# When tables are loaded and placed at the start of a fused Fourier mixer and feed-forward kernel

## The chip, the cores and the metric

The kernel runs on one core of a Trainium2 chip. The metric is the device time of one execution in microseconds. Before the change it is 861.91 us (median of three runs, 861.05 to 862.39). The core has five instruction streams that run side by side and wait for each other by semaphores: TensorE (matmul, "PE" in the profile), VectorE ("DVE"), ScalarE ("ACT"), GpSimd ("POOL") and SyncE ("SP"), which only issues transfers. GpSimd issues transfers too, among them those that convert 32-bit floats to 16-bit ones on the way. Sixteen DMA engines carry them all.

## What is computed

Two layers: a mixer that works in the frequency domain along the sequence, and a feed-forward network on its output.

```python
# x: (8, 3008, 256); w_r, w_i: (256, 256); b_r, b_i: (256,)
X = np.fft.rfft(x, axis=1)
Yr = Xr @ w_r - Xi @ w_i + b_r
Yi = Xr @ w_i + Xi @ w_r + b_i
Yr = sign(Yr) * maximum(abs(Yr) - 0.01, 0)     # the same for Yi
y = np.fft.irfft(Yr + 1j * Yi, n=3008, axis=1)
# then, on all 24064 rows; w_in: (256, 2048), w_out: (2048, 256); s, b: one number each
r = maximum(y @ w_in, 0)
out = (s * (r * r) + b) @ w_out
```

The kernel makes the Fourier transform of length 3008 = 94 x 32 out of matmuls with constant tables: a transform of length 94 (table A), one of length 32 with twiddle factors (table F, one 128 x 128 block for each of 24 pairs of frequencies), and, for the way back, one of length 32 (table T, 24 blocks too) and one of length 94 (table C).

## The kernel before

Image 0 is treated by a routine of its own, `first_batch`, which keeps all in on-chip memory. The later images go through units of work that are spread between the matmuls of the feed-forward network. A helper, `evac`, copies a PSUM tile to on-chip memory by ScalarE or VectorE, whichever has less to do by a running count. What comes first in the text comes first in each engine's stream, except where the scheduler of the language moves it.

The loads are issued in this order. `F_c` and `T_c` are the tables F and T as they lie in memory, 384 KB each; `F_t`, `F_2` and `T_t` are what the matmuls read, with zeros between the blocks.

```python
A_t = cpool.tile([P, 96], F16, name="A_t")
nc.sync.dma_start(out=A_t[0:N1, :], in_=A_d)
emit_load_x(0)                       # four chunks of image 0, issued by GpSimd, f32 -> f16
...                                  # w_st: w_r and w_i, 256 KB each, SyncE; b_g: four rows of 1 KB
F_c = uspool.tile([P, NPAIR, 2, N2], F16, name="F_c", tag="us")
nc.sync.dma_start(out=F_c.rearrange("p q r k -> p q (r k)"), in_=F_d)
...                                  # b_h: two rows, GpSimd
T_c = uspool.tile([P, NPAIR, 64], F16, name="T_c", tag="us")
nc.sync.dma_start(out=T_c, in_=T_d)
nc.sync.dma_start(out=sel_t, in_=S_d)
nc.sync.dma_start(out=eye_t, in_=E_d)
nc.sync.dma_start(out=C_t, in_=C_d)
b_st = rpool.tile([P, 2, D], F32, name="b_st", tag="rt")
for i, bv in enumerate((b_r, b_i)):
    nc.sync.dma_start(out=b_st[:, i], in_=bv.unsqueeze(0).to_broadcast([P, D]))
...                                  # s_bc, bb_bc
```

The pool of `b_st` and the two `w_st` has three buffers, which the feed-forward network's `rt` tiles use later. The small work and the placing of tables:

```python
def make_bounds():                   # GpSimd: low, high <- b_st
    for t, c in ((low, -LAM), (high, LAM)):
        nc.gpsimd.tensor_scalar(out=t, in0=b_st, scalar1=-1.0, scalar2=c, op0=ALU.mult, op1=ALU.add)

def make_w_g():                      # GpSimd: W_g <- w_st, used by images 1 to 7
    nc.gpsimd.tensor_tensor(out=W_g[:, :, 1], in0=w_st[1], in1=w_st[0], op=ALU.subtract)
    nc.gpsimd.tensor_tensor(out=W_g[:, :, 0], in0=w_st[1], in1=w_st[0], op=ALU.add)
    nc.gpsimd.tensor_scalar_mul(out=W_g[:, :, 0], in0=W_g[:, :, 0], scalar1=-1.0)

def place_f():
    for a in range(2):
        r = slice(64 * a, 64 * a + 64)
        nc.scalar.copy(out=blocks(F_t)[r, :, :, a], in_=F_c[r])
        for h, f in enumerate(F_2):
            q = slice(h * H, h * H + H)
            nc.vector.tensor_scalar_mul(out=blocks(f)[r, :, 0, a], in0=F_c[r, q, 1], scalar1=-1.0)
            nc.vector.tensor_copy(out=blocks(f)[r, :, 1, a], in_=F_c[r, q, 0])

def place_t():
    for i in range(4):
        r = slice(32 * i, 32 * i + 32)
        c = 64 * (i % 2)
        nc.vector.tensor_copy(out=T_t[r, :, c : c + 64], in_=T_c[r])
```

`first_batch` reads the chunks as they come, then runs twelve steps, (ec, u) with ec the half of the features and u = 0..5 (written (ec, u) = 0..11 in a row here):

```python
for c in range(N2 // XCH):           # 4 chunks
    for dc in range(DC):
        ...                          # 8 matmuls x16 x A_t -> psh   (L328)
        ...                          # two evac: one on ScalarE, one on VectorE -> ut
    keep_awake(18 if c < 3 else 12)  # matmuls on ones, to keep TensorE busy
    if c == 2:
        place_w()                    # ScalarE: W_t <- w_st
with tc.issue_after(last_dve.ins), tc.issue_after(last_act.ins):
    place_f()
    place_t()
gate = nc.gpsimd.tensor_copy(out=w_in_t[0][0:1, 0:1], in_=T_c[0:1, 0, 0:1])
with tc.issue_after(gate.ins):
    emit_load_x(1)
    emit_load_weights()              # w_in, w_out
...
def mix(ec, u):       # 8 matmuls ut x W_t -> psh (L367); then
    ...               # u % 3 == 1: g = copy on ScalarE (bias comes later, by a matmul with sel_t and b_h)
    ...               # else: g = psh + b_g on VectorE, the "bias add" (L377)
def fwd_dft(ec, u):   # 8 matmuls F_t, F_2 x g -> psf (L398); m on ScalarE (L403), z on VectorE (L405)
def inv_dft(ec, u):   # 4 matmuls z x T_t -> psa (L416); evac -> vt
...
for i in range(2 * U + 2):           # U = 6
    ...                              # mix(step i), fwd_dft(step i-1), inv_dft(step i-2)
    ...                              # from i = 8 on: turn, last_dft -> yt, and image 1's first stage
    if i == 6:
        make_w_g()
        make_bounds()
```

After that, the main loop runs the feed-forward network of all images (first matmul L702, relu L709 -> `rt`, square L713 or L716 -> `gt`, second matmul L771, last scaling L781), with the mixer's units of images 1 to 7 between.

Of the kernel before, what the change touches and what calls it, by code (L numbers as in the profile page):

```python
# [14 lines left out]
P = 128  # L15
# [79 lines left out]
def kernel(  # L95
# [13 lines left out]
    nc = tc.nc  # L109
    B, S, D = x.shape  # L110
# [5 lines left out]
    H = NPAIR // 2  # L116
# [5 lines left out]
    F_d = nc.inline_tensor(fwd.astype(np.float16), name="dft_fwd").ap()  # L122
    T_d = nc.inline_tensor(inv.astype(np.float16), name="dft_inv").ap()
    C_d = nc.inline_tensor(last.astype(np.float16), name="dft_last").ap()
# [3 lines left out]
    E_d = nc.inline_tensor(np.eye(P).astype(np.float16), name="identity").ap()  # L128
    S_d = nc.inline_tensor(sel.astype(np.float16), name="bias_sel").ap()
# [23 lines left out]
    def evac(dst, src, cols, scale=None):  # L153
        ta, td = 0.17 + cols / 1200.0, 0.15 + cols / 960.0
        if load["act"] + ta <= load["dve"] + td:
            load["act"] += ta
            if scale is None:
                return None, nc.scalar.copy(out=dst, in_=src)  # L158
            return None, nc.scalar.mul(out=dst, in_=src, mul=scale)
        load["dve"] += td  # L160
        if scale is None:
            return nc.vector.tensor_copy(out=dst, in_=src), None
        return nc.vector.tensor_scalar_mul(out=dst, in0=src, scalar1=scale), None

    def two_banks():
        return hpool.tile([P, 2, 512], F32, name="psh", tag="psh")
# [4 lines left out]
    def other_bank():  # L171
        return apool.tile([P, 512], F32, name="psa", tag="psa")
# [17 lines left out]
    def keep_awake(n):  # L190

        ps = other_bank()
        for _ in range(n):
            nc.tensor.matmul(ps[:, 0:P], ones, ones, start=True, stop=True)
# [15 lines left out]
        for i, bv in enumerate((b_r, b_i)):  # L210
            nc.sync.dma_start(out=b_g[r : r + 1, i], in_=bv.unsqueeze(0))
    F_c = uspool.tile([P, NPAIR, 2, N2], F16, name="F_c", tag="us")
    nc.sync.dma_start(out=F_c.rearrange("p q r k -> p q (r k)"), in_=F_d)
    b_h = cpool.tile([P, D], F16, name="b_h")
    nc.vector.memset(b_h, 0.0)

# [1 line left out]
        nc.gpsimd.dma_start(out=b_h[64 * i : 64 * i + 1], in_=bv.unsqueeze(0))  # L218
    sel_t = cpool.tile([P, P], F16, name="sel_t")
    T_c = uspool.tile([P, NPAIR, 64], F16, name="T_c", tag="us")  # L220
    nc.sync.dma_start(out=T_c, in_=T_d)

    nc.sync.dma_start(out=sel_t, in_=S_d)
    eye_t = cpool.tile([P, P], F16, name="eye_t")
    nc.sync.dma_start(out=eye_t, in_=E_d)
    C_t = cpool.tile([96, 96], F16, name="C_t")
    nc.sync.dma_start(out=C_t, in_=C_d)

    b_st = rpool.tile([P, 2, D], F32, name="b_st", tag="rt")
    for i, bv in enumerate((b_r, b_i)):  # L230
        nc.sync.dma_start(out=b_st[:, i], in_=bv.unsqueeze(0).to_broadcast([P, D]))
    low = cpool.tile([P, 2, D], F16, name="low")
    high = cpool.tile([P, 2, D], F16, name="high")
    W_g = cpool.tile([P, DC, 2, D], F16, name="W_g")
    s_bc = cpool.tile([P, 1], F32, name="s_bc")
    bb_bc = cpool.tile([P, 1], F32, name="bb_bc")
    nc.sync.dma_start(out=s_bc, in_=moe_s.unsqueeze(0).to_broadcast([P, 1]))
    nc.sync.dma_start(out=bb_bc, in_=moe_b.unsqueeze(0).to_broadcast([P, 1]))

    w_in_t = [cpool.tile([P, DFF], F16, name=f"w_in_{dc}") for dc in range(DC)]  # L240
    w_out_t = cpool.tile([P, MC, D], F16, name="w_out_t")
# [14 lines left out]
    T_t = cpool.tile([P, NPAIR, P], F16, name="T_t")  # L256
    nc.vector.memset(T_t, 0.0)
    F_2 = [uspool.tile([P, H, P], F16, name="F_2", tag="us") for _ in range(2)]
# [3 lines left out]
    def make_bounds():  # L262
        for t, c in ((low, -LAM), (high, LAM)):
            nc.gpsimd.tensor_scalar(
                out=t, in0=b_st, scalar1=-1.0, scalar2=c, op0=ALU.mult, op1=ALU.add
            )

    def make_w_g():
# [6 lines that stand above are left out]
    def blocks(t):  # L275
        return t.rearrange("p q (r a k) -> p q r a k", r=2, a=2)

    def place_w():
        for i in range(2):
            nc.scalar.copy(out=W_t[:, :, i], in_=w_st[i])  # L280

    def place_f():
        for a in range(2):
            r = slice(64 * a, 64 * a + 64)
            nc.scalar.copy(out=blocks(F_t)[r, :, :, a], in_=F_c[r])

            for h, f in enumerate(F_2):
                q = slice(h * H, h * H + H)
                nc.vector.tensor_scalar_mul(
                    out=blocks(f)[r, :, 0, a], in0=F_c[r, q, 1], scalar1=-1.0  # L290
                )
                nc.vector.tensor_copy(out=blocks(f)[r, :, 1, a], in_=F_c[r, q, 0])

    def place_t():
        for i in range(4):
            r = slice(32 * i, 32 * i + 32)
            c = 64 * (i % 2)
            nc.vector.tensor_copy(out=T_t[r, :, c : c + 64], in_=T_c[r])  # L298

    def make_bias():  # L300
        ps = other_bank()
# [17 lines left out]
    def first_batch():  # L319
        ut = ypool.tile([P, DC, 96, N2], F16, name="ut", tag="yt")  # L320
        last_dve = last_act = None
        keep_awake(44)
        for c in range(N2 // XCH):
            for dc in range(DC):
                ps = two_banks()
                for j in range(XCH):
                    lo = j * D + dc * P
                    last_pe = nc.tensor.matmul(  # L328
                        ps[:, j // 4, (j % 4) * 96 : (j % 4) * 96 + 96],
                        x16[(0, c)][0:N1, lo : lo + P], A_t[0:N1, :],  # L330
                        start=True, stop=True,
                    )
                for h in range(2):
                    n2 = c * XCH + 4 * h
                    on_dve, on_act = evac(
                        ut[:, dc, :, n2 : n2 + 4],
                        ps[:, h, 0:384].rearrange("p (n k) -> p k n", k=96), 384,
                    )
                    last_dve = on_dve or last_dve
                    last_act = on_act or last_act  # L340
            with tc.issue_after(last_pe.ins):
                keep_awake(18 if c < 3 else 12)
            if c == 2:
                with tc.issue_after(last_act.ins):
                    place_w()
        with tc.issue_after(last_dve.ins), tc.issue_after(last_act.ins):
            place_f()
            place_t()

        gate = nc.gpsimd.tensor_copy(out=w_in_t[0][0:1, 0:1], in_=T_c[0:1, 0, 0:1])  # L350
        with tc.issue_after(gate.ins):
# [5 lines left out]
        vt = bigpool.tile([P, DC, N2, 96], F16, name="vt", tag="corr")  # L357
        gs = {}
        zt = {}
        g_last = [None]  # L360

        def mix(ec, u):
            ps = two_banks().rearrange("p h (j r e) -> p (h j) r e", j=2, r=2)
            for j in range(4):
                q = 4 * u + j
                for dc in range(DC):
                    nc.tensor.matmul(  # L367
                        ps[:, j], ut[:, dc, 4 * q : 4 * q + 4, :],
                        W_t[:, dc, :, ec * P : (ec + 1) * P],
                        start=(dc == 0), stop=(dc == DC - 1),  # L370
                    )
            g = vpool.tile([P, 4, 2, P], F16, name="g0", tag="v")
            if u % 3 == 1:
                nc.scalar.copy(out=g, in_=ps)
                load["act"] += 1.02
            else:
                g_last[0] = nc.vector.tensor_tensor(  # L377
                    out=g, in0=ps,
                    in1=b_g[:, :, ec * P : (ec + 1) * P].unsqueeze(1).to_broadcast([P, 4, 2, P]),
                    op=ALU.add,  # L380
                )
                load["dve"] += 1.2
            gs[(ec, u)] = g
# [77 lines left out]
        def some(n):  # L461
            for _ in range(n):
                if more:
                    more.pop(0)()

        steps = [(ec, u) for ec in range(DC) for u in range(U)]
        for i in range(2 * U + 2):
            if i < 2 * U:
                mix(*steps[i])
            if 0 <= i - 1 < 2 * U:  # L470
                fwd_dft(*steps[i - 1])
            if 0 <= i - 2 < 2 * U:
                inv_dft(*steps[i - 2])
            k = i - U - 2
            if 0 <= k < 4:
                turn(0, k)
            if 0 <= k - 1 < 4:
                last_dft(0, 8 * (k - 1))
            if i >= 2 * U:
                some(3)  # L480
            if i == 6:
                make_w_g()
                make_bounds()
        for k in range(4):
            turn(1, k)
            some(1)
# [307 lines left out]
    def schedule(start, span, units):  # L794
        for i, u in enumerate(units):
            plan.setdefault(start + (i * span) // len(units), []).append(u)

    more = first_batch()
    load.update(act=0.0, dve=0.0)
    mark = {}  # L800
# [8 lines left out]
    for b in range(2, B):  # L809
        s0, s1, s2 = mark[b - 2], mark[b - 1], mark[b]  # L810
        p = s1 - s0
        schedule(s0 + 40, p - 48, s1_units(b))
        p = s2 - s1
# [47 lines left out]
```

## Time and profile before

| What | Value |
|---|---|
| Time, median of three | 861.91 us |
| Span in the profile | 860.5 us |
| PE busy | 839.1 us, 98% |
| PE weight loads busy | 604.3 us, 70% |
| DVE busy | 699.4 us, 81% |
| ACT busy | 642.8 us, 75% |
| POOL busy | 33.2 us, 4% |
| DMA moved | 95.07 MB, mean 110 GB/s |

The busy table is a sum over the whole span. The page's second part cuts the span in 40 slices of 21.5 us and gives each engine's busy share in tenths, TensorE's granted clock and the load of the DMA engines. The chain is followed back from the last instruction, at each step to what released it. A timeline row reads: start in us, length in us, engine, line of the program, operation, output<-inputs, count, and in brackets the idle time before with what ended it.

### The profile page before, as it was taken

How to read it: one execution, taken by the hardware profiler on the slowest of the kernel's cores; microseconds unless marked ns; L12 is line 12 of the kernel's file. 1: busy time of each engine (PE TensorE's matmuls, PEld its weight loads, DVE VectorE, ACT ScalarE, POOL GpSimd, SP SyncE). 2: the span in 40 equal slices, each digit the busy share in tenths (PEclk: the TensorE clock that was granted, in tenths of full speed). 3: DMA queues.
4: the chain of work that ended last, by engine and by line, in shares of the span. 5: the costliest groups of instructions: out<-in, count | busy, mean ns of one | idle time of the engine just before them, and what ended most of it. 6: DMA issues, size and time to landing. Idle time of an engine off the chain costs nothing.

```text
span 860.5 us, 17125 instructions
## 1 busy us (share of the span) xinstructions
PE 839.1 (98%) x6690; PEld 604.3 (70%) x6690; DVE 699.4 (81%) x1019; ACT 642.8 (75%) x856; POOL 33.2 (4%) x53
## 2 busy tenths in 40 slices
PE   6889999999999999999999999999999999999996
PEld 6666776777777766777667776777767777766665
DVE  6688997888878887888878888888977888776664
ACT  4587887777877887778777877788877787766662
POOL 4110000000000000000000000000000000000000
PEclk9899999999999999999999999999999999999999
DMA  8845266423673357423664246713354223411111
GB/s 183 138 93 144 77 150 179 141 69 70 157 179 110 84 136 179 141 73 75 169 157 115 76 108 166 193 42 94 102 154 117 63 77 96 111 32 38 37 40 53
DMA packets 104866, 95.07 MB, mean 110 GB/s; under 512 B 9422, under 2 KB 97234, under 8 KB 103442
## 3 DMA queue, kind: packets, MB, share of 16 engines
q1 hardware_dynamic: 98786, 79.57, 31.9%
q0 software_dynamic: 6000, 14.42, 10.4%
q8 instruction: 52, 0.85, 0.4%
q14 instruction: 28, 0.23, 0.1%
HBM read 52.54 MB, written 46.66 MB: 115 GB/s over the span
## 4 chain that ended last, share of the span: by engine, by line
PE 89%; DVE 4%; ACT 3%; DMA 2%; issue 1%; SPq 0%; POOL 0%; DVEq 0%; POOLq 0%
PE psh L702 36%; PE psa L771 36%; PE psf L568 4%; PE psf L503 3%; PE psf L539 2%; PE psf L554 2%; PE psf L598 2%; PE psf L651 2%; DMA x<-in_x_dram 1%; DVE gt L716 1%; ACT rt L709 1%; PE psh L367 1%; DVE T_t L298 1%; ACT yt L158 1%; ACT m L403 0%
## 5 line engine op out<-in xcount | busy, mean ns | idle before, releaser
L709 ACT ACTIVATE rt<-psh 128x1024 f32<-128x1024 f32 (+2 forms) x384 | 387.1, 1009 | 117.0 <-PE psh L702 115.8
L716 DVE TENSOR_TENSOR gt<-rt 128x1024 f16<-128x1024 f32 (+2 forms) x323 | 386.2, 1198 | 101.0 <-ACT rt L709 100.4
L771 PE MATMUL psa<-w_out_t,gt 128*128 128x256 f16 (+1 forms) x3024 | 453.9, 272 | 0.1
L771 PEld LDWEIGHTS <-gt 128*128 128x128 f16 (+1 forms) x3024 | 301.1, 101 | 186.9 <-issue 1.7
L702 PE MATMUL psh<-yt,w_in 128*128 128x512 f16 (+1 forms) x1344 | 396.9, 378 | 0.0
L702 PEld LDWEIGHTS <-w_in 128*128 128x128 f16 x1536 | 142.8, 98 | 26.6 <-issue 1.7
L781 DVE SCALAR_TENSOR_TENSOR ost<-psa,s_bc,bias_bc 128x512 f32<-128x512 f32 (+1 forms) x96 | 70.8, 737 | 8.1 <-PE psa L771 5.7
L713 ACT ACTIVATE gt<-rt 128x1024 f16<-128x1024 f32 (+2 forms) x61 | 64.3, 1054 | 1.0
L573 DVE TENSOR_TENSOR ring<-psf,s 128x512 f16<-128x512 f32 x84 | 57.4, 683 | 3.5 <-PE psf L568 3.3
L158 ACT CAST v<-psf 128x512 f16<-128x512 f32 x80 | 46.5, 582 | 18.1 <-PE psf L598 18.1
L158 ACT CAST xf<-psf 128x512 f16<-128x512 f32 x82 | 48.0, 585 | 11.1 <-PE psf L539 11.1
L158 ACT CAST u<-psf 96x512 f16<-96x512 f32 x78 | 45.1, 580 | 12.3 <-PE psf L503 12.1
L702 PE MATMUL psh<-tail,w_in 128*128 128x512 f16 (+1 forms) x192 | 52.1, 353 | 0.0
L568 PE MATMUL psf<-W_g,xf 128*128 128x256 f16 x336 | 50.4, 273 | 0.0
L158 ACT CAST yt<-psf 128x480 f16<-128x480 f32 (+2 forms) x76 | 38.5, 518 | 14.4 <-PE psf L651 14.4
L503 PE MATMUL psf<-x,A_t 94*96 94x512 f16 x104 | 39.6, 381 | 1.7 <-ACT yt L158 0.5
L579 DVE TENSOR_TENSOR ring<-ring,high 128x512 f16<-128x512 f16 x84 | 35.5, 422 | 2.2
L580 DVE TENSOR_TENSOR ring<-ring 128x512 f16<-128x512 f16 x84 | 35.4, 421 | 1.9
L578 DVE TENSOR_TENSOR ring<-ring,low 128x512 f16<-128x512 f16 x84 | 35.3, 421 | 1.5
L568 PEld LDWEIGHTS <-xf 128*128 128x128 f16 x336 | 32.9, 98 | 3.7
L182 POOL DMA_DIRECT2D x<-in_x_dram x32 | 16.7, 524 | 482.3 <-PE psf L503 445.1
L651 PE MATMUL psf<-C_t,vs 96*128 96x96 f16 x448 | 32.9, 205 | 0.0
(80 smaller groups left out, 496.9 us busy)
## 6 DMA issues: line engine op xcount, KB each, us to landing
out_dram<-ost SPq DMA_DIRECT2D x152, 128.0 KB
x<-in_x_dram POOLq DMA_DIRECT2D x32, 376.0 KB, 6.0
ud<-u SPq DMA_DIRECT2D x28, 384.0 KB
us<-ud SPq DMA_DIRECT2D x28, 384.0 KB
vd<-v SPq DMA_DIRECT2D x42, 256.0 KB
vs<-vd SPq DMA_DIRECT2D x14, 768.0 KB
ring<-ring SPq DMA_DIRECT2D x280, 32.0 KB
out_dram<-ost SPq DMA_DIRECT2D x16, 120.0 KB
```

The costliest lines, as they stand in the source:

```text
L158: return None, nc.scalar.copy(out=dst, in_=src)
L503: nc.tensor.matmul(ps[0:96, :], A_t[0:N1, :], x16[(b, c)][0:N1, j * D : (j + 2) * D], start=True, stop=True,)
L568: nc.tensor.matmul(ps[:, r, :], xt[:, 2 - r, dc], W_g[:, dc, r], start=(dc == 0), stop=(dc == DC - 1),)
L573: nc.vector.tensor_tensor(out=t, in0=ps, in1=hold[i // 2][:, i % 2].unsqueeze(1).to_broadcast([P, 2, D]), op=ALU.add,)
L579: nc.vector.tensor_tensor(out=m, in0=m, in1=high, op=ALU.min)
L651: nc.tensor.matmul(ps[:, j * 96 : (j + 1) * 96], vs[(b, h)][:, k, ec * P : (ec + 1) * P], C_t, start=True, stop=True,)
L702: nc.tensor.matmul(o, w_in_t[dc][:, mc * P : (mc + 1) * P], r, start=(dc == 0), stop=(dc == DC - 1),)
L709: nc.scalar.activation(out=rt[:, :, 0:w], in_=ps[:, :, 0:w], func=AF.Relu)
L713: nc.scalar.activation(out=gt[:, :, 0:w], in_=rt[:, :, 0:w], func=AF.Square)
L716: nc.vector.tensor_tensor(out=gt[:, :, 0:w], in0=rt[:, :, 0:w], in1=rt[:, :, 0:w], op=ALU.mult)
L771: nc.tensor.matmul(ps[0:size, h, :], gts[(ti, mc // 2)][:, mc % 2, sub * size : (sub + 1) * size], w_out_t[:, mc, :], start=(mc == 0), sto ...
L781: nc.vector.scalar_tensor_tensor(out=ost[0:size, 0:k], in0=ps[0:size, 0:k], scalar=s_bc[0:size], in1=bias_bc[0:size, 0:k], op0=ALU.mult, o ...
```

## The change

The loads of F and T no longer start at once. A one-element clear of `F_c` on VectorE, put behind its casts of chunk 1, stands ahead of F's load, and one of `T_c` behind its casts of chunk 2 ahead of T's and of all the small loads that follow: a transfer that overwrites a cleared element has to wait for the clear. So the chunks of the first image meet fewer other transfers. The tables F_2 and T_t are placed in halves: the first half of F_2 ahead of the first bias add, the first half of T_t behind it, and the second halves behind the next bias add on VectorE. `F_t` is still placed at once, by ScalarE. GpSimd's `make_w_g` and `make_bounds` move from step 6 to step 9, behind a one-element copy that reads `vt`, so that the scheduler can't pull them forward.

```diff
-    nc.sync.dma_start(out=F_c.rearrange("p q r k -> p q (r k)"), in_=F_d)
-    nc.sync.dma_start(out=T_c, in_=T_d)
-    nc.sync.dma_start(out=sel_t, in_=S_d)
-    ... (loads of eye_t, C_t, b_st, s_bc, bb_bc)
+    def emit_load_forward():
+        nc.sync.dma_start(out=F_c.rearrange("p q r k -> p q (r k)"), in_=F_d)
+        nc.sync.dma_start(out=sel_t, in_=S_d)
+
+    def emit_load_inverse():
+        t_load = nc.sync.dma_start(out=T_c, in_=T_d)
+        with tc.issue_after(t_load.ins):
+            ... (loads of eye_t, C_t, b_st, s_bc, bb_bc)
@@ place_f: the F_2 part is taken out
+    def place_f_2(h):
+        q = slice(h * H, h * H + H)
+        for a in range(2):
+            r = slice(64 * a, 64 * a + 64)
+            nc.vector.tensor_scalar_mul(out=blocks(F_2[h])[r, :, 0, a], in0=F_c[r, q, 1], scalar1=-1.0)
+            nc.vector.tensor_copy(out=blocks(F_2[h])[r, :, 1, a], in_=F_c[r, q, 0])
-    def place_t():
+    def place_t(h):
+        q = slice(h * H, h * H + H)
         for i in range(4):
             r = slice(32 * i, 32 * i + 32)
             c = 64 * (i % 2)
-            nc.vector.tensor_copy(out=T_t[r, :, c : c + 64], in_=T_c[r])
+            nc.vector.tensor_copy(out=T_t[r, q, c : c + 64], in_=T_c[r, q])
@@ first_batch, in the loop over the chunks
+            if c == 1:
+                with tc.issue_after(last_dve.ins):
+                    nc.vector.memset(F_c[0:1, 0, 0, 0:1], 0.0)
+                emit_load_forward()
+            if c == 2:
+                with tc.issue_after(last_dve.ins):
+                    nc.vector.memset(T_c[0:1, 0, 0:1], 0.0)
+                emit_load_inverse()
@@ after it
             place_f()
-            place_t()
+            place_f_2(0)
@@ in the loop over the steps
-            if i == 6:
-                make_w_g()
-                make_bounds()
+            if i == 0:
+                with tc.issue_after(g_last[0].ins):
+                    place_t(0)
+            if i == 2:
+                with tc.issue_after(g_last[0].ins):
+                    place_f_2(1)
+                    place_t(1)
+            if i == 9:
+                gate = nc.gpsimd.tensor_copy(out=low[0:1, 0, 0:1], in_=vt[0:1, 1, 0, 0:1])
+                with tc.issue_after(gate.ins):
+                    make_w_g()
+                    make_bounds()
```

The built program differs from the one before in the order of the first rows of VectorE, in a few groups of TensorE's in image 0 and in when SyncE and GpSimd issue; ScalarE's order is the same.

More of the change, by code (lines that the diff above doesn't have):

```diff
@@ L220 @@
     T_c = uspool.tile([P, NPAIR, 64], F16, name="T_c", tag="us")
-    nc.sync.dma_start(out=T_c, in_=T_d)
-    nc.sync.dma_start(out=sel_t, in_=S_d)
     eye_t = cpool.tile([P, P], F16, name="eye_t")
-    nc.sync.dma_start(out=eye_t, in_=E_d)
     C_t = cpool.tile([96, 96], F16, name="C_t")
-    nc.sync.dma_start(out=C_t, in_=C_d)
     b_st = rpool.tile([P, 2, D], F32, name="b_st", tag="rt")
-    for i, bv in enumerate((b_r, b_i)):
-        nc.sync.dma_start(out=b_st[:, i], in_=bv.unsqueeze(0).to_broadcast([P, D]))
     low = cpool.tile([P, 2, D], F16, name="low")
@@ L236 @@
     bb_bc = cpool.tile([P, 1], F32, name="bb_bc")
-    nc.sync.dma_start(out=s_bc, in_=moe_s.unsqueeze(0).to_broadcast([P, 1]))
-    nc.sync.dma_start(out=bb_bc, in_=moe_b.unsqueeze(0).to_broadcast([P, 1]))
+    def emit_load_forward():
[4 more added lines that the diff above has]
+        with tc.issue_after(t_load.ins):
+            nc.sync.dma_start(out=eye_t, in_=E_d)
+            nc.sync.dma_start(out=C_t, in_=C_d)
+            for i, bv in enumerate((b_r, b_i)):
+                nc.sync.dma_start(out=b_st[:, i], in_=bv.unsqueeze(0).to_broadcast([P, D]))
+            nc.sync.dma_start(out=s_bc, in_=moe_s.unsqueeze(0).to_broadcast([P, 1]))
+            nc.sync.dma_start(out=bb_bc, in_=moe_b.unsqueeze(0).to_broadcast([P, 1]))
     w_in_t = [cpool.tile([P, DFF], F16, name=f"w_in_{dc}") for dc in range(DC)]
@@ L285, in place_f @@
             nc.scalar.copy(out=blocks(F_t)[r, :, :, a], in_=F_c[r])
[L287 to L292, printed above, removed]
-    def place_t():
+    def place_f_2(h):
+        q = slice(h * H, h * H + H)
+        for a in range(2):
+            r = slice(64 * a, 64 * a + 64)
+            nc.vector.tensor_scalar_mul(
+                out=blocks(F_2[h])[r, :, 0, a], in0=F_c[r, q, 1], scalar1=-1.0
+            )
+            nc.vector.tensor_copy(out=blocks(F_2[h])[r, :, 1, a], in_=F_c[r, q, 0])
+    def place_t(h):
+        q = slice(h * H, h * H + H)
         for i in range(4):
```

## The prediction, made before the changed kernel ran

> **What bounds the kernel now.** I read first the busy table by slices and the shares of the chain that ended last, then the busy time by stage, then the chain and the timelines inside the first 30 us. The first two, from the page:
>
> ```profile
> PE   6889999999999999999999999999999999999996
> ...
> PEclk9899999999999999999999999999999999999999
> ...
> PE 89%; DVE 4%; ACT 3%; DMA 2%; issue 1%; SPq 0%; POOL 0%; DVEq 0%; POOLq 0%
> ```
>
> TensorE is full in all but the first two slices (21.5 us each) and the last, and the chain runs through it for 89%. The same by stage (us in the stage; then busy us and instruction count of PE, PE weight loads, DVE, ACT and GpSimd; granted clock; DMA share; GB/s):
>
> ```profile
> 0.00:17.40 17.40, 12.36 (x175) 11.22 (x175) 9.00 (x17) 6.47 (x12) 5.98 (x15) 1.00 0.78 186
> 17.40:25.00 7.60, 2.35 (x19) 1.82 (x20) 7.40 (x13) 3.13 (x3) 7.59 (x9) 0.91 1.03 187
> 25.00:60.00 35.00, 31.93 (x369) 25.65 (x369) 27.09 (x37) 26.55 (x43) 1.73 (x3) 0.92 0.53 95
> 60.00:860.50 800.50, 792.51 (x6130) 565.59 (x6127) 655.95 (x954) 606.67 (x800) 17.90 (x28) 1.00 0.41 109
> ```
>
> From 60 us on TensorE is busy 792.5 of 800.5 us. The edit touches nothing there. From 17.4 to 25.0 TensorE works 2.35 of 7.60 us, while VectorE works 7.40 and GpSimd 7.59. What is saved ahead of 60 us moves the whole PE-bound rest forward by as much, if the order of work stays. Now the chain of waits (start, length, what):
>
> ```profile
> 2.87 12.36 DMA x<-in_x_dram
> 15.27 0.53 PE psh L328 x8
> ...
> 19.00 0.55 DVE T_t L298
> 19.56 1.67 DVE T_t L298
> 21.24 1.51 DVE T_t L298
> 22.77 0.88 DVE T_t L298
> 23.68 1.24 DVE g L377
> 24.95 1.01 PE psf L398 x8
> ```
>
> Two things set this stage: the four chunks of image 0, the last usable at 15.27 us, and the T_t copies, behind which the first bias add (g, L377) waits in VectorE's order. The PE timeline gives the chunks: their matmuls begin at 6.33, 9.07, 11.97 and 15.27, so 2.74, 2.90 and 3.30 us apart. The GpSimd timeline says why four equal copies took 0.55 to 1.67 us:
>
> ```profile
> 19.66 1.19 POOL L247 DMA_DIRECT2D w_out_t<-in_moe_w_out_dram  x1
> 20.86 1.48 POOL L272 TENSOR_TENSOR W_g<-w_st 128x512 f16<-128x512 f32 x1
> 22.33 0.90 POOL L264 TENSOR_SCALAR low<-b_st 128x512 f16<-128x512 f32 x1
> ```
>
> Copies two, three and four end 0.37, 0.41 and 0.42 us after the ends of these three rows (20.85, 22.34, 23.23). Each seems to wait for a GpSimd instruction and then to need about 0.4 us itself.
>
> **What the Trainium skill says.** "SBUF — State Buffer", section "Who interferes with whom": VectorE in a 2-port mode (SBUF-to-SBUF copies) and GpSimd share one pair of ports as an exclusive lock; whoever comes second waits for the whole instruction, while a VectorE instruction with at most one SBUF input outside those modes is not touched. The trace agrees: the ends above, and the bias add at 23.68, beside GpSimd work, took 1.23 us against 1.22 elsewhere. "DMA: Bandwidth & Descriptors", section "Queues, rings and completion order": each DMA engine goes round-robin over the queues that have work, so tables on SP's queue take turns with x on GpSimd's. The growing chunk distance agrees. Same page, "Anatomy of one DMA — SWDGE (gpsimd) path": about 2 us are fixed per transfer; I use this, as an estimate, for the tables too, whose landings this trace doesn't list. "TensorE: Matmul & The Clock Gate", section "What's actually happening": after a window with TensorE idle (about 3.4 us) the clock halves. The trace agrees: after a gap of 3.85 us (21.10 to 24.95) the clock from 24 to 30 us is 0.50, and eight L398 matmuls take 1.01 us instead of 0.46 at 31 us.
>
> **The change, part by part.** *1. Tables behind the chunks.* When chunk 1 is read at 9.07 us, A_t, the 512 KB of w_st and two chunks have moved: 1.31 MB in the 6 us since about 3, at 244 GB/s (3 to 9 us) little short of all that fits. So F_c came after; I leave chunk 1 at 9.05. Later chunks no longer share. From 21 to 24 us, where only image 1's chunks move, the rate is 205 GB/s; a chunk is 94 x 4,096 bytes = 385 KB, so 1.9 us. Chunk 2: 10.95; chunk 3: 12.85, and 0.35 for F_c's first packets: 13.2 instead of 15.27, a gain of 2.1.
>
> F_c is gated by a one-element clear behind VectorE's chunk-1 casts, which ended at 11.16. Issue at 11.25, 2 us fixed, 393 KB at 265 GB/s (9 to 12 us) 1.5: landing at 14.7. ScalarE's last cast ends 1.41 after chunk 3's matmuls start (15.27 to 16.68 before), so at 14.6. The F_t copies (2.95 us, both) then run 14.7 to 17.65, ending 1.85 sooner. T_c, gated one chunk later (VectorE done at 13.05), lands near 16.6, against 15.73 or before; GpSimd's loads of image 1 and the FFN weights start 1 us later. Image 1 is first multiplied at 51.2 us and its loads and w_in, w_out end by 37, so that costs nothing.
>
> *2. Halves behind bias adds.* VectorE's last ut cast ends 2.09 after chunk 3 starts: 15.3. Before, eight F_2 operations (17.28 to 18.98, 1.70 us) and T_t (4.65) stood ahead of the first add. Now four F_2 operations: 0.85, to 16.15. The first mix (8 x 0.107 us and the latency to read PSUM, 1.0) is ready at 16.3. VectorE's order is then, worked from row durations (add 1.22, less 0.08 overlap when back to back; z 0.68; half a T_t without interference, 4 x 0.25 = 1.0 from the 0.4 for a full-width copy; half F_2 0.85):
>
> g0 16.3–17.5; T_t half 17.5–18.5; z0 waits for F_t (17.65), 0.46 of warm L398, ScalarE's g1 (17.65–18.6) and m (0.69): 19.3–20.0; g2 20.0–21.2; z1 –21.9; F_2 half –22.75; T_t half –23.8; g3 –25.0; z2 –25.7; z3 waits for g3's L398 and m: 26.3–27.0; g5 at 27.0.
>
> Before, g5 started at 34.68. The gain is 7.7 us. The 1.85 us of tables in the middle and the two halves' fixed costs fit where VectorE formerly waited (2.17 us before the second add, 0.81 and 1.29 before z2 and z3). From g5 on, VectorE has the same list in both kernels and the later waits, for PSUM and ScalarE, are of the same kind. Cross-check at the first L398 group: it ended at 25.97 and now at 18.1, 7.9 less. Of it, 2.1 are chunks, 0.55 the warm clock, and 5.2 the tables no longer ahead.
>
> *3. GpSimd.* Five operations (1.26, 1.48, 0.90, 1.78, 0.61: 6.03 us) move behind the first vt of the second half, formerly at 40.67, now near 33: to about 39. They release the buffers that the first rt (60.49 before, 53 after) takes, so 14 us remain. VectorE works there on PSUM inputs, which the 1.23 us add shows to be undisturbed. Cost: nothing. W_g is first used at 79.4 us.
>
> Sum: 861.9 – 7.7, and 0.2 held back for a T_t half meeting the weights' descriptor writing on GpSimd: 854.4.
>
> **Rivals.** *A, the chunks gain nothing,* because their own queue, not sharing, sets the 3 us. For: the chunks' queue shows only 205 to 216 GB/s even when alone (21 to 30 us). Against: alone it brings a chunk in 1.9 us, and 2.90 and 3.30 grow just when F_c and T_c move. Then F_t ends at 19.5 as before, the first L398 at 20.0, the gain is 5.5 to 6: about 856.2. *B, the tables become the wait.* F_c, issued 8 us later than before, is needed at once; each us of delay past 14.7 moves F_t and the chain one for one. T_c has 0.9 us of slack before the first T_t half, then blocks VectorE's whole queue. For: little slack, and an estimated fixed cost. With both 2 us late the gain is about 5.5, with 3.5 us late 4: 856.4 to 858. *C, VectorE becomes the bound* from 17 to 27 us, with the halves slowed as in the old trace (to 1.5 us a copy). The second half lies after 22.7 when GpSimd's descriptors are done (near 21.5), so only the first is exposed, by 1 to 2 us, of which 0.8 is slack: 855 to 856. *D, more gain:* F_c early and no interference: the L398 group at 17.2, 8.5 to 9 us in all: 853. *E, the rest takes it back:* nothing in 792.5 of 800.5 us busy points to that beyond a us, since TensorE's order differs only before image 0 is half through.
>
> **Range and chances.** A, B and C share the low end of the gain and D the other: 851.6 to 857.6 holds 8 in 10. Two per cent are 17.2 us. All that stands ahead of 25 us besides data arrival is less than that, so a 2% gain has a chance of 0.01; a 2% loss needs a new stall in the long stage: 0.02. Within 2%: 0.97.
>
> **What would show it.** Right: chunk matmuls at about 9, 11 and 13.2; F_t copies from 14.7; first bias add near 16.3; first L398 near 17.7; T_t halves of about 1 us; no half-clock stretch after 21 us; first L702 near 50.3 (57.98 before); the stage after it as long as before. Wrong: chunk 3 still near 15 (A); a wait of F_t or T_t for its load (B); T_t copies of over 0.5 us (C); a gain at first L702 that isn't in the total (E).

## The result, and the profile after

The changed kernel takes 855.31 us (median of four runs, 855.22 to 855.38), the kernel before 862.1 us (four runs beside it, 861.05 to 862.39). The ratio is 0.9923, 95% interval 0.9906 to 0.9941: a gain of 0.8%, some 6.6 us (5.1 to 8.1 by the interval). The prediction said 854.4 us, a gain of 7.5, range 851.6 to 857.6, within 2%.

The page of the changed kernel, its slices, TensorE's clock and the shares of the chain:

```profile
PE   7899999999999999999999999999999999999996
...
PEclk9999999999999999999999999999999999999999
...
PE 89%; DVE 4%; ACT 3%; DMA 2%; issue 1%; SPq 1%; POOL 0%; DVEq 0%; ACTq 0%; POOLq 0%
```

The first and the third slice are a tenth fuller (before: 6889...), and the second slice's clock is 9 instead of 8 tenths. The stages (columns as in the prediction):

```profile
0.00:17.40 17.40, 13.26 (x190) 11.78 (x190) 11.01 (x24) 8.21 (x13) 3.57 (x11) 1.00 0.82 181
17.40:25.00 7.60, 5.64 (x60) 4.54 (x61) 6.58 (x16) 5.63 (x8) 4.38 (x7) 1.00 0.89 163
25.00:60.00 35.00, 31.65 (x347) 23.20 (x346) 30.07 (x41) 29.69 (x47) 7.53 (x10) 1.00 0.78 149
60.00:853.50 793.50, 785.46 (x6095) 561.93 (x6093) 649.95 (x947) 599.30 (x790) 16.86 (x26) 1.00 0.40 108
```

From 17.4 to 25.0 us TensorE now works 5.64 us (2.35 before), at full clock. The best marker is the first matmul of the feed-forward network, L702 before and L728 now: 57.98 us before, 50.89 after, 7.09 earlier. From there to the end of the span it is 802.5 us before and 802.6 after: the long stage neither gives nor takes. Line numbers moved with the edit: the group L398 of the kernel before is L414 here, and it keeps its old name in the text. The chain in the first 30 us (start, length, what):

```profile
1.87 7.06 DMA x<-in_x_dram
8.98 0.53 PE psh L336 x8
9.53 0.49 ACT ut L158
10.04 1.02 DVE ut L162 x2
11.12 3.73 DMA F_c<-dft_fwd
14.93 1.47 ACT F_t L289
16.42 1.47 ACT F_t L289
17.91 1.01 ACT g L390
...
22.87 0.35 DVE T_t L306
23.23 0.35 DVE T_t L306
23.60 0.35 DVE T_t L306
23.96 0.36 DVE T_t L306
24.35 1.24 DVE g L393
```

It no longer runs through chunk 3, but from chunk 1 over F's gated load (3.73 us from issue to use) to ScalarE's copies into F_t; later, T_t's second half stands in VectorE's way. The chunk matmuls start at 6.82, 8.98, 11.00 and 12.99 us.

### The profile page after: what moved, and what is told of

Same layout as the page of the kernel before. It is cut to its first block, busy times and chain, and to the rows that moved or that the text cites. A ratio compares the mean times of both kernels' runs of the same rounds, so it can differ in the third digit from the quotient of the medians.

```text
span 853.5 us, 17135 instructions
## 1 busy us (share of the span) xinstructions
PE 836.0 (98%) x6690; PEld 601.4 (70%) x6690; DVE 697.6 (82%) x1025; ACT 642.8 (75%) x856; POOL 32.3 (4%) x54
## 4 chain that ended last, share of the span: by engine, by line
PE 89%; DVE 4%; ACT 3%; DMA 2%; issue 1%; SPq 1%; POOL 0%; DVEq 0%; ACTq 0%; POOLq 0%
PE psh L728 36%; PE psa L797 36%; PE psf L594 4%; PE psf L529 3%; PE psf L565 2%; PE psf L580 2%; PE psf L677 2%; PE psf L624 2%; DVE gt L742 1%; DMA out_dram<-ost 1%; DMA x<-in_x_dram 1%; ACT rt L735 1%; DVE g L393 1%; ACT yt L158 1%; DMA F_c<-dft_fwd 0%
## 5 line engine op out<-in xcount | busy, mean ns | idle before, releaser
L728 PE MATMUL psh<-yt,w_in 128*128 128x512 f16 (+1 forms) x1344 | 397.3, 378 | 0.0
L728 PEld LDWEIGHTS <-w_in 128*128 128x128 f16 x1536 | 142.7, 98 | 26.6 <-issue 1.7
L728 PE MATMUL psh<-tail,w_in 128*128 128x512 f16 (+1 forms) x192 | 52.2, 353 | 0.0
L182 POOL DMA_DIRECT2D x<-in_x_dram x32 | 16.7, 525 | 461.2 <-PE psf L529 445.1
```

Of the source, the lines that this page charges most:

```text
L728: nc.tensor.matmul(o, w_in_t[dc][:, mc * P : (mc + 1) * P], r, start=(dc == 0), stop=(dc == DC - 1),)
```

## The experiments

Each run's time is a median beside runs of the kernel before on the same chip (860.94 to 861.61 us by group). Beside it stands the start of the first feed-forward matmul in its profile ("first FFN"), which leaves out the scatter of the long stage but is one execution. The changed kernel, run again as the measure for the others:

> The changed kernel once more, beside the others of this group on the same chip: 855.0 to 855.8, first feed-forward matmul at 50.9 us in the profile. It is the measure for the runs below.

Measured: 855.29 us (855.15 to 855.36), ratio 0.9932 (0.9919 to 0.9944), first FFN 50.94.

### One part undone at a time

**Whole tables in front.** The halves are undone, gates and GpSimd's move stay.

```diff
             place_f()
             place_f_2(0)
+            place_f_2(1)
+            place_t_all()            # four copies of 32 x 1536, as before
@@ the calls at i == 0 and i == 2 are taken out
```

> The changed kernel, but all of F_2 and all of T_t are placed ahead of the first bias add, as before the change. My theory: eight F_2 operations (1.7 us) and four whole T_t copies of about 0.55 us, with no GpSimd work to wait for, put the first bias add near 19.1 us instead of 16.1 and the first L398 near 20.4 instead of 17.9; but the second halves no longer stand between later adds, so that most of this is made up again by the sixth add, and the time is only 0.5 to 1.2 us above the changed kernel, 855.8 to 856.5. Rival 1, the placement in halves is the main part of the gain: 3 us or more above it, 858.3 or more. Rival 2, only transfers and GpSimd matter: equal to it within 0.3 us.

Measured: 857.09 us (six executions, 855.27 to 858.16; 0.9950; 0.9936 to 0.9963), first FFN 52.43. The first bias add is at 19.13 and the first L398 group at 20.41, as expected, but the time is 1.8 us above the changed kernel, between my theory and rival 1; only two of the six executions, 855.27 and 855.58, lost next to nothing. The stages of 3 us show what I had left out:

```profile
18.00:21.00 3.00, 1.08 (x11) 0.88 (x11) 2.31 (x3) 1.03 (x2) 3.00 (x7) 0.94 0.93 84
21.00:24.00 3.00, 3.00 (x21) 2.24 (x18) 1.68 (x2) 1.08 (x2) 1.02 (x1) 0.50 1.05 199
```

TensorE waited 2.37 and 0.81 us between 16.7 and 20.4 us, and its clock (third column from the right) was then 0.50.

**No gates.** Loads as before the change, halves and GpSimd's move stay.

```diff
-            if c == 1: (clear of F_c, emit_load_forward())
-            if c == 2: (clear of T_c, emit_load_inverse())
@@ ahead of first_batch
+    nc.sync.dma_start(out=F_c.rearrange("p q r k -> p q (r k)"), in_=F_d)
+    nc.sync.dma_start(out=T_c, in_=T_d)
+    ... (sel_t, eye_t, C_t, b_st, s_bc, bb_bc)
```

> The changed kernel, but F_c, T_c and the small loads are issued at the start, as before the change. My theory, tables and chunks share the DMA engines: chunk matmuls again about 2.9 to 3.3 us apart, chunk 3 near 15.3 instead of 13.0, F_t done near 19.6 instead of 17.9, the first L398 1.7 us later, and as much in the time: 856.7 to 857.3. Rival, the chunks are set by their own queue, and the change's 2.0 us distances come from something else: chunks stay about 2.0 us apart and the time is that of the changed kernel, 855.3.

Measured: 856.77 us (856.54 to 858.34; 0.9954; 0.9941 to 0.9966), first FFN 53.37. The TensorE timeline:

```profile
9.16 0.85 PE L346 MATMUL psh<-A_t,x 94*128 94x96 f16 x16 [1.00 <-DMA x<-in_x_dram]
11.60 0.85 PE L346 MATMUL psh<-A_t,x 94*128 94x96 f16 x16 [0.58 <-DMA x<-in_x_dram]
15.26 0.85 PE L346 MATMUL psh<-A_t,x 94*128 94x96 f16 x16 [1.79 <-DMA x<-in_x_dram]
```

Chunk 3 is back at 15.26, with the chunks 2.86, 2.44 and 3.66 us apart. That it comes at 12.99 in the changed kernel is due to the gates, and rival A falls. In this execution the clock also fell, to 0.59 and 0.56 in the two stretches from 16 to 20 us, so its 2.4 us on first FFN hold some clock too; the median is 1.5 us above the changed kernel.

**GpSimd's work where it was.**

```diff
-            if i == 9:
-                gate = nc.gpsimd.tensor_copy(out=low[0:1, 0, 0:1], in_=vt[0:1, 1, 0, 0:1])
-                with tc.issue_after(gate.ins):
-                    make_w_g()
-                    make_bounds()
+            if i == 6:
+                make_w_g()
+                make_bounds()
```

> The changed kernel, but W_g, low and high are made where they were (step 6, with nothing to hold them back). In the built program the three W_g operations then stand ahead of the gate for image 1's loads, in time in which GpSimd idles, and only low and high follow the loads. My theory: W_g costs nothing there, low and high (1.5 us, near 22 us) meet the second half of T_t and make it wait for up to 1 us: 855.3 to 856.3. Rival, moving GpSimd's work is a large part of the gain whatever else is changed: 2 us or more above the changed kernel, 857.3 or more.

Measured: 857.43 us (six executions, 855.68 to 858.08; 0.9950; 0.9937 to 0.9964), first FFN 52.82: 1.9 to 2.1 us above the changed kernel, more than my theory has it and as much as the rival, though two of the six executions, 855.68 and 855.89, lie in my theory's range. VectorE's timeline:

```profile
22.04 0.61 DVE L296 TENSOR_SCALAR F<-F_c 64x384 f16<-64x384 f16 x1
22.58 0.66 DVE L299 COPY F<-F_c 64x384 f16<-64x384 f16 x1
23.26 0.26 DVE L296 TENSOR_SCALAR F<-F_c 64x384 f16<-64x384 f16 x1
```

Two copies of F_2, not of T_t, took 0.61 and 0.66 instead of 0.25 us, beside `low` and `high` on GpSimd (21.89 and 22.48, 0.65 each). The next bias add came at 25.18 instead of 24.35, 0.8 later, about as expected. But then the clock fell, where the changed kernel has 1.00:

```profile
24.00:27.00 3.00, 1.03 (x9) 0.83 (x9) 2.93 (x6) 0.50 (x1) 0.00 (x0) 0.83 1.06 212
27.00:30.00 3.00, 3.00 (x28) 2.39 (x26) 1.70 (x2) 1.29 (x3) 0.00 (x0) 0.60 1.07 216
```

By first FFN the wait of 0.8 us had become 1.9. I put the rest down to the clock; no run of this kernel with the clock held shows it.

### GpSimd and the clock by themselves

**The kernel before with GpSimd's work moved, nothing else** (the edit is the reverse of the last).

> The kernel before, with only GpSimd's W_g, low and high moved behind the first vt of the second half. My theory, T_t's copies waited for GpSimd's instructions: the four copies take about 0.55 us each, 2.2 us in all instead of 4.65 (one more us if one of them meets the descriptor writing of w_out), the first bias add starts near 21.2 instead of 23.7, and TensorE's gap falls below the length at which its clock halved, which is worth up to 1 us more: 858.3 to 859.8. Rival, the copies are slow by themselves or through the transfers: 4.65 us as before and 862.

Measured: 859.20 us (0.9975; 0.9966 to 0.9983), first FFN 54.99. VectorE:

```profile
17.87 1.00 DVE L289 TENSOR_SCALAR F<-F_c 64x384 f16<-64x384 f16 x1
...
19.42 2.25 DVE L298 COPY T_t<-T_c 32x1536 f16<-32x1536 f16 x4
```

The four copies take 2.25 us, 0.56 each, instead of 4.65: they had waited for GpSimd. One F_2 operation took 1.00 us and ended 0.07 us after GpSimd's issue of w_out's load (17.60 to 18.80): the issue of a load can stand in the way too. TensorE's gap shrank to 2.09 us, yet the clock was 0.50 from 25 to 27 us. That part of my expectation failed. The first bias add came at 21.69 instead of 21.2.

**The kernel before with matmuls on ones in the gap.**

```diff
             if i < 2 * U:
                 mix(*steps[i])
+            if i == 1:
+                with tc.issue_after(mix_pe[0].ins):     # the last matmul of this mix
+                    keep_awake(74)
```

> The kernel before, with 74 matmuls on ones put between the second mix and the first L398 group, so that TensorE doesn't idle for 3.85 us there; they feed nothing. My theory, part of the gain is TensorE's clock: the clock from 24 to 30 us is 1.0 instead of 0.5, the eight L398 take 0.46 us instead of 1.01, the second and third bias adds on VectorE come 0.5 to 2 us earlier, the first feed-forward matmul at 56.2 to 57.3 instead of 57.98, the time 859.5 to 860.7. Rival, VectorE sets the pace there and the clock doesn't matter: the same as before, 861.3, within 0.3.

Measured: 859.43 us (0.9981; 0.9974 to 0.9987), first FFN 55.55. T_t's copies still take 4.66 us and the first bias add is at 23.59, but:

```profile
24.00:27.00 3.00, 2.37 (x31) 1.90 (x28) 1.58 (x3) 0.69 (x1) 1.49 (x2) 1.00 1.05 210
27.00:30.00 3.00, 3.00 (x37) 2.61 (x37) 3.00 (x4) 2.32 (x4) 0.00 (x0) 1.00 1.03 206
```

The kernel before has half the clock in the same stretches:

```profile
24.00:27.00 3.00, 2.04 (x14) 1.72 (x14) 0.90 (x1) 0.69 (x1) 1.59 (x2) 0.50 1.06 213
27.00:30.00 3.00, 3.00 (x19) 2.22 (x17) 2.51 (x3) 0.69 (x1) 0.00 (x0) 0.50 1.08 216
```

Useless work on TensorE, and nothing else, brings 2.0 us of time (1.7 by the means of all executions) and 2.4 of first FFN, more than I had expected. The second and third bias adds on VectorE came 0.2 and 1.5 us earlier. In this execution the clock was low at another place, 0.62 and 0.82 in the stretches from 15 to 21 us, behind a wait of 1.98 us for chunk 3; there VectorE set the pace, whose table copies ended only at 23.55.

**Both together.**

> The kernel before, with GpSimd's W_g, low and high moved (the run with that alone had its first feed-forward matmul at 54.99 us, a halved clock from about 24 to 28) and 40 matmuls on ones behind the second mix. It differs from the run with whole tables, gates and 56 such matmuls (51.26) only by the gates of the loads. My theory, what is left is the share of the chunks' earlier landing, 2.3 us: clock 1.0 throughout, first feed-forward matmul at 53.2 to 54.0, time 857.5 to 858.5. Rival, the clock and GpSimd's work are the same time counted twice (either of them alone fills the gap): 54.8 to 55.2 as with one of them alone.

Measured: 858.05 us (0.9963; 0.9951 to 0.9976), first FFN 53.87, clock 1.00 from 15 us on. The two together bring 4.1 us of first FFN, more than either alone (2.4 and 3.0), so the rival falls; but alone they sum to 5.4, so that some of the time is in both.

**Whole tables in front, with matmuls on ones.** The first run of the section before, "One part undone at a time", with `keep_awake(56)` behind the second mix.

> The changed kernel with whole tables ahead of the first bias add (the earlier run), plus 56 matmuls on ones behind the second mix. In the earlier run the first L398 came 2.5 us later than in the changed kernel, the first feed-forward matmul 1.5 us later, and the clock was halved from 21 to 24 us. My theory, of these 1.5 us about 1 is the halved clock and the rest the order: no halved clock, first feed-forward matmul at 51.2 to 51.8 (changed kernel 50.9), time 0.3 to 0.9 us above the changed kernel. Rival, all is VectorE's order: 52.4, time 1.5 us above it.

Measured: 855.53 us (855.33 to 855.80; 0.9935; 0.9922 to 0.9947), first FFN 51.26. The first L398 group is at 20.58 us, 2.6 later than in the changed kernel, and all but 0.3 us of it is made up by first FFN. With the clock held, placing the tables in halves is worth 0.2 to 0.3 us.

These make a row in which each kernel differs from the one before it by one part, apart from the number of matmuls on ones (74, 40 and 56, as much as each gap takes):

| Kernel | Time, us | First FFN, us | Step in time | Step in first FFN |
|---|---|---|---|---|
| Before (beside the next) | 861.39 | 57.98 | | |
| + matmuls on ones (clock) | 859.43 | 55.55 | –2.0 | –2.4 |
| + GpSimd's work moved | 858.05 | 53.87 | –1.4 | –1.7 |
| + gates | 855.53 | 51.26 | –2.5 | –2.6 |
| halves in place of the matmuls on ones | 855.29 | 50.94 | –0.2 | –0.3 |

(57.98 is from an execution of 862.33 us, near the top of that kernel's 860.1 to 862.9; so the last column sums to 7.0, the medians to 6.1. The third time is from another chip; the kernel before had 860.94 there. Taken against the kernel before on the same chip, the steps in the median are 2.0, 0.9, 3.0 and 0.2 us, those in the mean of all executions 1.7, 1.5, 2.8 and 0.3. The shares hold for this order.)

### A better version

**F_t in halves.**

```diff
-    def place_f():
+    def place_f(h):
+        q = slice(h * H, h * H + H)
         ...
-            nc.scalar.copy(out=blocks(F_t)[r, :, :, a], in_=F_c[r])
+            nc.scalar.copy(out=blocks(F_t)[r, q, :, a], in_=F_c[r, q])
@@ place_f(0) in place of place_f(); m_last[0] holds the last m; in the loop over the steps
             if i == 2:
+                with tc.issue_after(m_last[0].ins):
+                    place_f(1)
```

> The changed kernel, with F_t placed in halves too: the first half (1.6 us) ahead of ScalarE's first g, the second behind its second m. My theory, F_t's 2.95 us on ScalarE are on the chain from F's load to the first L398: this group starts near 17.4 instead of 17.9, ScalarE's g and m of the first steps 0.9 to 1.3 us earlier, the first feed-forward matmul 0.5 to 0.9 us earlier than in the changed kernel, and the time as much lower. Rival, VectorE's adds and table halves from 16 to 25 us are the bound, and ScalarE is beside it: no difference beyond 0.2 us.

Measured: 854.95 us (854.70 to 856.62; 0.9934; 0.9922 to 0.9947), first FFN 50.37, 0.5 earlier. The first L398 group is at 16.94. In the time the ranges of the two kernels overlap, so by the time alone it is unclear.

**Then T_t's second half later, or on GpSimd.**

```diff
             if i == 2:
                 with tc.issue_after(g_last[0].ins):
                     place_f_2(1)
-                    place_t(1)
+            if i == 3:
+                with tc.issue_after(z_last[0].ins):     # z_last[0] holds the last z
+                    place_t(1)
```

> The changed kernel with F_t in halves (first feed-forward matmul at 50.37 us), and the second half of T_t (1.45 us) no longer ahead of the fourth step's bias add but behind the third step's z, where VectorE waits 0.8 us. My theory, this add and what follows come 1.45 us earlier and give back 0.6 to 0.8: first feed-forward matmul at 49.4 to 49.9, time 854.0 to 854.6. Rival, the chain runs through ScalarE and TensorE there by now: 50.4 and 854.9, no difference.

Measured: 853.77 us (853.03 to 854.11; 0.9912; 0.9896 to 0.9927), first FFN 49.40. The copies ran from 24.09 to 25.53 us, in what had been a wait of VectorE, and the fourth step's bias add came at 22.35 instead of 23.68.

In the other version they stay at i == 2, with `nc.gpsimd.tensor_copy` for `nc.vector.tensor_copy`:

> The changed kernel with F_t in halves, and the second half of T_t copied by GpSimd behind its descriptor writing (from about 21.7 us). My theory: VectorE loses 1.45 us of work on its chain, GpSimd's four copies take 0.8 to 0.9 us each and end near 25.2, and VectorE's second F_2 half waits for up to 0.9 us by the shared ports: first feed-forward matmul 0.3 to 1.2 us earlier than 50.37. Rival: the scheduler, which takes GpSimd for slow, has put the second half's inverse transforms later in TensorE's and ScalarE's order, which costs more than is gained: 50.5 to 52.

Measured: 856.44 us (0.9950; 0.9935 to 0.9965), first FFN 51.66. GpSimd's four copies took 3.55 us from 21.45 on, as estimated, and the fifth bias add on VectorE came 0.2 us earlier than with F_t in halves; the seventh came 1.4 us later, since several inverse transforms stand later in TensorE's order. VectorE's second F_2 half took 2.2 us instead of 0.85, which is more wait than the 0.9 that I had allowed. The rival was right. That it is the scheduler's estimate of GpSimd's speed that moved them is my reading and wasn't tried.

**And w_out's load later.**

```diff
+            if i == 5:
+                gate = nc.gpsimd.tensor_copy(out=w_out_t[0:1, 0, 0:1], in_=vt[0:1, 0, 0, 48:49])
+                with tc.issue_after(gate.ins):
+                    emit_load_w_out()        # taken out of emit_load_weights
```

> The kernel with F_t in halves and T_t's second half later (first feed-forward matmul at 49.40 us), with the load of w_out held back on GpSimd until the fourth step's vt (about 26 us). In that kernel one F_2 copy of the second half took 0.94 us instead of 0.25 and ended 0.08 us after GpSimd's issue of w_out (20.60 to 21.79). My theory, VectorE's copies wait for the issue of a load on GpSimd too when it writes many descriptors: the copy takes 0.25 us, the next bias add starts 0.6 to 0.7 us earlier, the first feed-forward matmul at 48.7 to 49.2, time 853.0 to 853.6. Rival, the copy was slow by another cause (it reads what arrives, or ScalarE reads the same table beside it): 0.9 us again, and 49.4.

The F_2 copy in question on VectorE and the issue of w_out on GpSimd, without w_out's later load, then the copy with it:

```profile
20.60 1.19 POOL L251 DMA_DIRECT2D w_out_t<-in_moe_w_out_dram  x1
20.93 0.94 DVE L300 COPY F<-F_c 64x384 f16<-64x384 f16 x1
```

```profile
21.21 0.24 DVE L302 COPY F<-F_c 64x384 f16<-64x384 f16 x1
```

Measured: 853.30 us (853.12 to 853.36; 0.9903; 0.9886 to 0.9920), first FFN 48.97. The next bias add came 0.4 us earlier (21.93 instead of 22.35). It is the fastest version, 2.0 us below the changed kernel, on another chip (8.3 us below the kernel before there, against 6.1).

## Why the prediction was right, and where it was off

**The chunks** were right: 9.05, 10.95 and 13.2 predicted, 8.98, 11.00 and 12.99 measured, and the run without gates shows the cause: the tables' loads among the chunks made the distances of 2.9 and 3.3 us, and without them a chunk takes 2.0. That they do so by taking turns on the DMA engines is the prediction's reading; no run sets it apart.

**F's load and F_t.** Landing at 14.7 was predicted; ScalarE waited 0.53 us for it and began at 14.93, so F_t was done at 17.88 and not 17.65. The first L398 group started at 17.94 (17.7).

**The halves** are the term of the sum that was mis-sized. The first bias add came at 16.11 (16.3 predicted), but a T_t half took 1.53 and 1.45 us, not "1.0 from the 0.4 for a full-width copy":

```profile
17.25 1.53 DVE L306 COPY T_t<-T_c 32x768 f16<-32x768 f16 x4
19.67 0.69 DVE L421 SCALAR_TENSOR_TENSOR z<-psf,m 128x512 f16<-128x512 f32 x1 [0.88 <-ACT m L419]
22.87 1.45 DVE L306 COPY T_t<-T_c 32x768 f16<-32x768 f16 x4
```

Undisturbed full copies take 0.56 us each and halves 0.36; by these two sizes a copy has a part of about 0.16 us that doesn't shrink with its width. I had read the 0.4 us left after GpSimd's ends as the whole copy. The first half's excess cost nothing: VectorE still waited 0.88 us behind it. The second half's 0.45 us counted. It began 0.1 us late, and the fourth step's bias add came 0.55 late (24.35 instead of 23.8), the sixth step's (g5) at 27.60 instead of 27.0 and first FFN at 50.89 instead of 50.3: the 0.6 us that the hand sum was too low by. Another 0.4 of the 0.9 us between 854.4 and 855.3 comes from taking a gain read in an execution of 862.33 us off the median of 861.9; the 0.2 held back works the other way.

**GpSimd** was right in the new place: it worked from 34.22 to 39.63 (33 to 39 predicted) and nobody waited for it. The interference for which 0.2 us were held back didn't show in this kernel: T_t's first half took 1.53 us beside the issue of image 1's loads, the second 1.45 with GpSimd idle. It was w_out's issue that could block a copy, and in the changed kernel that had just ended (21.92) when the second F_2 half began at 22.00. That was luck: in the next version, with F_t in halves, a copy came earlier and was caught.

**The cross-check's shares were wrong, though the sum nearly held** (the end of the first L398 group came 7.4 us earlier, from 25.96 to 18.56, and not 7.9). I gave "2.1 chunks, 0.55 the warm clock, and 5.2 the tables no longer ahead". The row above, in its several countings, gives the clock 1.7 to 2.4, GpSimd's work 0.9 to 1.7, the gates 2.5 to 3.0 and the halves as such 0.2 to 0.3. The 0.55 counted one group of eight matmuls; the mixes and the groups after it ran at half clock too, until 30 us, and the second and third bias adds waited for them. The halves' use in the change is above all that TensorE no longer idles: with whole tables and no matmuls on ones 1.8 us are lost, with them 0.2.

**The rivals.** A fell. B was real but small: the F_t wait of 0.53 us; T_t waited for nothing, though with 0.2 us to spare and not 0.9 (GpSimd, which waits for the same load, went on at 17.02, and T_t's first copy began at 17.25). C came true in part, by the copies' fixed part and not by GpSimd; no copy of a half took over 0.5 us. D didn't come. E fell: 802.5 and 802.6 us after the first FFN. One reading was off as well: by the digits TensorE was below 9 tenths in the first three slices of the kernel before, not the first two.

## What to carry to other kernels

When a start-up stage feeds a long bound stage, mark the first instruction of the long stage: what it gained here, the span gained. A gap of TensorE can cost more than its length, when the stage after it runs at half clock, and matmuls that feed nothing show how much of a gain that is. Place table copies into waits that VectorE has anyway, away from GpSimd's arithmetic and from its issue of a load like w_out's.

## What the runs showed that I had not expected

- GpSimd's issue of w_out (1.19 to 1.20 us) held up a VectorE copy of F_2 in four experiments until 0.07 to 0.09 us after its end (0.94 to 1.00 us instead of 0.25), and holding back the load removed that. It did not hold every copy: in five experiments one that began in the first 0.2 us of the issue took its usual 0.23 or 0.24 us. The issues of image 1's and w_in's loads, 0.5 to 0.6 us each, had copies of 0.24 to 0.38 us beside them. Which property of w_out's load makes the difference wasn't tried.
- A VectorE copy of 32 partitions from 16-bit to 16-bit took 0.36 us for 768 columns and 0.56 for 1,536.
- The clock fell after gaps well short of the 3.85 us in the kernel before. In the run with GpSimd's work moved alone, two gaps of 1.38 and 2.09 us came before 0.50; in the run without gates, a single one of 1.79 us before chunk 3, behind keep-awake matmuls, before 0.59. But the length of a gap alone doesn't decide it, as three traces show.

The run with matmuls on ones alone waited 1.98 us for chunk 3, and its clock from 15 to 18 us was 0.62:

```profile
15.19 1.04 PE L328 MATMUL psh<-A_t,x 94*128 94x96 f16 x16 [1.98 <-DMA x<-in_x_dram]
15.00:18.00 3.00, 2.81 (x32) 2.62 (x33) 1.75 (x6) 2.21 (x3) 1.84 (x5) 0.62 0.47 48
```

The run with both parts waited as long at the same place, and its clock stayed at 1.00:

```profile
15.24 0.85 PE L328 MATMUL psh<-A_t,x 94*128 94x96 f16 x16 [1.98 <-DMA x<-in_x_dram]
15.00:18.00 3.00, 2.43 (x35) 2.02 (x36) 1.70 (x6) 2.21 (x3) 2.00 (x5) 1.00 0.65 58
```

With F_t in halves it stayed at 1.00 behind a gap of 2.91 us:

```profile
24.96 0.22 PE L416 MATMUL psf<-g,F_t 128*128 128x128 f16 x1 [2.91 <-DVE g L395]
24.00:27.00 3.00, 2.04 (x27) 1.79 (x27) 2.18 (x4) 1.16 (x2) 0.00 (x0) 1.00 1.06 212
```

What else decides it stays open; it may differ between executions of one kernel. The three kernels whose longest gap from 7 us on is 0.76 to 1.10 us repeated within 0.2 to 0.5 us. Of the ten with gaps of 1.41 to 3.85 us, nine scattered by 1.1 to 3.4 us and one (with 1.98 and 1.76 us) by 0.2. Only one execution of each was traced, so that the clock makes this scatter isn't shown.
